# Two more pairs with P split and turned by the DMA, and the softmax sums turned with the last slot of P, in an attention and convolution kernel

## The chip, the cores and the metric

The kernel runs on one core of a Trainium2 chip. The metric is the device time of one execution in microseconds (us), as the median of three runs; lower is better. The engines are PE (matmul; PEld is its weight load), DVE, ACT and POOL (elementwise), and SP, which here only issues DMAs.

## What is computed

```python
q_n, k_n = rmsnorm(q, g_q), rmsnorm(k, g_k)            # 8 batches, 12 heads, 448 positions, 64 wide
scores = (q_n @ k_n.T) / sqrt(64)
attn = exp(scores - max(scores, -1))
attn = attn / (sum(attn, -1) + 1e-9)
x = (attn @ v) -> (8, 448, 768)                        # heads side by side
h = max(x @ w_in, 0)                                   # 768 -> 1024
conv = sum of 3 taps of conv_w over positions of h
out = (h * sigmoid(conv)) @ w_out                      # 1024 -> 768, float32
```

## The kernel before, in words

**Pairs.** The 96 heads are taken two at a time: pairs 0 to 47, six to a batch. For each pair, q and k are loaded, squared, summed, normalised (`rsqrt`, `apply_rms`) and turned; `scores` are multiplied into PSUM banks in seven slots of 128 query rows. For every slot `soft_max` (DVE, L999) takes the negated row maximum into a small tile, and `soft_exp` (ACT, L1007) writes P = exp(...) in float32 into one of four buffers `e`, and the row sum into a column of `rsum` (128 rows, 7 columns).

**Two ways for P.** P has to be turned before it can be multiplied with v. For a pair below `NV` = 10 it stays in float32: `p_transpose` (PE, L1038) turns each slot by four multiplications with the identity, 112 columns each; `p_evac` (a float32 copy, mostly on ACT, L438) moves it from the bank into `PT`; and `pv` (PE, L1120) multiplies in float32, eight products that PE carries out as 16 MATMULs. From pair `NV` on six of the seven slots (`TURNS`) are split into two float16 parts, `p_hi` (a cast) and `p_lo` (the rest, a subtraction on POOL or DVE, L450), in one of four buffers `ph`, and `p_turn` (SP, L1030) turns both by one DMA transpose. The last slot is still turned on PE, and then taken apart by `p_evac` (a cast) and `p_low` (DVE, L1055). Also v is split, by `v_hi` (mostly ACT) and `v_lo` (DVE, L1105), into `vp`, and `pv` takes three passes of eight products in float16, 24 MATMULs. `x_scale` then multiplies with the inverted sums: two instructions a pair on DVE below `NV` (L1134), one from there on (L1131).

**The sums.** After the last `soft_exp` of a pair, `sum_add` adds 1e-9 (POOL or DVE), `sum_step` inverts (DVE, L1065), `sum_transpose` (PE, L1068) turns the 128 x 7 tile into a bank of its own, `sum_evac` copies it to `rT`, and DMAs store it to DRAM (`sum_store`) and load it back, spread over the partitions (`sum_load`), as `rB`.

**The second half.** For each batch, `in_part` (PE, L1201) multiplies x, split in two float16 parts, with w_in; `in_relu`, `in_conv`, `in_tanh` and `in_gate` work on the bank (ACT and DVE); `in_hi` and `in_lo` split the result; `out_part` (PE, L1270) multiplies with w_out. The weights arrive as 64-bit numbers and are made into float32 in three DVE instructions a piece (`convert`), bounded (`bound`), and split (`split`, `rest`), all in the first part of the program.

**What sets the order.** Every step of the program has a number in a hand-held table (`ORDER`), and an engine for each elementwise step in another (`ENGINES`); `BANKS` names the PSUM bank of each step that takes one. The steps are issued in the order of the numbers, so each engine works through its own list in that order, without reordering. A step that waits holds up everything behind it on its engine.

Of the kernel before, what the change touches and what calls it, by code (L numbers as in the profile page):

```python
# [20 lines left out]
NF, NV, NQ = 10, 10, 10  # L21
# [10 lines left out]
    load_cw="3=6e4j",  # L32
    make_cw="8(",
    load="02080K0N0u0;0|1e1k2I2j2-2>3O4T4Y5D5Q5)626a6p7G7O7(868Z8v",
    convert=(
        "0A0D0G0g0i0t0!0)0-0}131S1P1Z1f1v1$1}1?2V2f2a2i2)2c2$42353a452}3P3^3h3r3|4C4F4O4A4D4I4<53"
        "5851555E5r5x5$5v5_5}6L6Q6W6f6i6l6|767B797E7J7p7w7!7*7}828K8O8T8j8l8q8`91999B9D9J"
    ),
    bound="0J0$0?2~2M2B2@2^4E4B44497q6X6d7T7L7k7<8h7)7n8a8e98969F9O",
    bound_max="4H9R",  # L40
    bound_turn="4J9U",
    bound_row="4L9X",
    bound_spread="4Q9i",
    scale="4S9l",
    in_factor="7N",
    split="4Z4o4*4~5p5(9p9y9<A5AKAsA<B8",
    rest="4i4w4^5a5y6Y9u9&9`ABARA$B2Bq",
    out_factor="A!",
    load_k=(
        "00040T0q1M2F2<3-4a5s6J7j7~9+AzCMDRElFuG-IKJXKnMCNIOGPvQ#R@T4UmVjWWY5Z$anbrcoe!fSgwh!j>j~"  # L50
        "mRmwo|p3"
    ),
    load_q=(
        "030B0a0#1t2R3j464d5+6=7m8^9>A&CQD_EyG6G`I#JjK*MGN`OUP@Q&SgTIU?VlX8YBZ(aqcScre%fVg|h&j_k3"
        "mqm!p0p7"
    ),
    square=(
        "060E0O0j151c2p2*4G4X606Z7>8A9tATCtC~E|FFGsHkJ_KXL%MuObO=R9RTTGTzVqW1YOYoapb6c;dHfRf<hfiD"
        "kVkkm_n9pTpb"
    ),  # L60
    square_sum=(
        "070I0b0p1G1j2+2?4V4n6E6u898YAHAmD0D6FEFZHfHwKaKhMAM!OkO{RKRdTYT*V;WIYYYva(bFdAdPfyg1hliL"
        "khkrnJnSpepo"
    ),
    rsqrt=(
        "090C0F0H0L0P0R0U0W0M0Q0S0V0X0c0f0h0k0d0m0o0s0y0&0*0<110x0z0(0+0=0_101A1E1s1u1y1#1%1;1=1^"
        "222{2|3033363D3F3I3f4t4v4x4(4-4=4@5B5F6(6+6<6?6{6}737M7R8g8k8o8s8x8$8+8=90A#A+A;A~B1BFBP"
        "BVBhDCDLDUDXDpDtDyD!D&FiFqFsF&F)F<F@F^F}H-H@H`H}I4ILITIdIhKtKuKwK&K_K~L1L7LDM;M=M?M_M|N1"
        "N2NENHP6PAPDPFPUPWPdPgPlRkRoRxR(R-R=R?R_S7T@T_T|U0U4U5U9UAUHWRWVWYWkWlWqWuW%W*Y=Y?Y_Y}Y~"
        "Z0Z2Z5Z7bNbPbSbfbhbibmbobsdXdadddmdzd%d?d_d`g8gCgFgKgLgOgQgUgYiSiViYiaibifigijipk!k#k&k*"  # L70
        "k=k@k_l7l9nZnandngnknlnnnqnvptpvpzp#p;p@p`q3q7"
    ),
# [73 lines left out]
    sum_store=(
        "2N3N3t5M5~6$7g8bAfBfD4DxF8GIHtIyJ@L9M3NLO;P$ROScTyU%W5X6YJZnazbQc<eEf+h8h=i}kBlimVoAo_qG"
# [1257 lines left out]
```

## Time and profile before

| what | value |
|---|---|
| median of three runs | 804.49 us (804.42 to 805.22) |
| the profiled execution's own time | 805.12 us |
| its span, first to last instruction | 803.3 us |
| PE busy | 780.5 us (97%) |
| DVE busy | 712.0 us (89%) |
| ACT busy | 637.5 us (79%) |
| POOL busy | 450.7 us (56%) |
| DMA queue that SP fills | 79.9% of 16 engines' span |
| granted TensorE clock | 0.998 |

The span is what the profile shows; the 1.8 us between it and the time lie around it. Busy shares are means over the whole program, and the stages differ: the weights are prepared in the first fifth, attention goes on to about 700 us, and the last 60 us belong to the second half of the last batch. Matmuls overlap, so the mean duration of one is longer than what it adds to the stream; busy time over the number of instructions, or the distance from one start to the next, is nearer to that.

### The profile page before, as it was taken

To read this page: it belongs to the slowest core of one execution; us is meant where nothing else is said; L and a number is where in the kernel's file an instruction comes from. 1 tells how busy PE (TensorE), PEld (TensorE's weight loads), DVE (VectorE), ACT (ScalarE), POOL (GpSimd) and SP (SyncE) were. 2 spreads that over 40 slices of the span, in tenths; PEclk is the share of its full clock that TensorE was granted. 3 is DMA by queue.
4 is the path that set the end of the run, shared out by engine and by line. 5 is a ranking of instruction groups with operands and counts; after the bars stand their busy time and mean duration, and the time that the engine had idled before them with its cause. 6 is when DMAs were issued, how large, how long until landed. Compare 5 with 4: busy or idle time off the path is not lost.

```text
span 803.3 us, 16861 instructions
## 1 busy us (share of the span) xinstructions
PE 780.5 (97%) x5564; PEld 421.6 (52%) x5564; DVE 712.0 (89%) x1489; ACT 637.5 (79%) x1542; POOL 450.7 (56%) x552
## 2 busy tenths in 40 slices
PE   3998999999999999999999999999999999999998
PEld 1545555555554555555555555555555555555554
DVE  7999999999999889998899988999999899992560
ACT  5999999997898777998788868998799767862221
POOL 2556246766478457766696646885487543530020
PEclk9999999999999999999999999999999999999999
DMA  8864653499998989999899999999999998846002
GB/s 246 236 193 116 172 179 101 97 186 208 187 199 183 195 177 209 194 182 195 188 188 199 200 181 199 207 190 197 191 189 180 209 196 182 160 91 150 12 1 79
DMA packets 345704, 137.46 MB, mean 171 GB/s; under 512 B 285376, under 2 KB 342032, under 8 KB 345616
## 3 DMA queue, kind: packets, MB, share of 16 engines
q1 hardware_dynamic: 345616, 136.37, 79.9%
q8 instruction: 44, 0.72, 0.4%
q14 instruction: 44, 0.36, 0.1%
HBM read 56.65 MB, written 11.18 MB: 84 GB/s over the span
## 4 chain that ended last, share of the span: by engine, by line
PE 55%; DVE 1%; ACT 1%; issue 1%; POOL 0%; ACTq 0%
PE bank L1270 21%; PE bank L1201 17%; PE bank L1120 7%; PE bank L993 7%; PE bank L1038 1%; PE bank L812 1%; ACT e L1007 0%; PE bank L1068 0%; DVE c L1221 0%; DVE ph L450 0%; POOL ph L450 0%; ACT PT L438 0%; ACT ph L438 0%; ACT sq L741 0%; ACT bank L1209 0%
## 5 line engine op out<-in xcount | busy, mean ns | idle before, releaser
L1201 PE MATMUL bank<-x,wi 128*128 128x448 f16 x1152 | 236.6, 353 | 0.8 <-DVE c L1231 0.6
L450 POOL TENSOR_TENSOR ph<-e,ph 128x448 f16<-128x448 f32 x139 | 148.8, 1073 | 93.9 <-ACT ph L438 60.9
L1270 PE MATMUL bank<-wo,gring 128*128 128x384 f16 (+1 forms) x1056 | 191.7, 327 | 0.0
L1201 PEld LDWEIGHTS <-wi 128*128 128x128 f16 x1152 | 110.1, 98 | 102.0 <-issue 12.8
L1270 PEld LDWEIGHTS <-gring 128*128 128x128 f16 (+1 forms) x1056 | 100.4, 99 | 65.1 <-issue 10.8
L993 PE MATMUL bank<-kT,qT 64*128 64x448 f16 (+3 forms) x1072 | 128.1, 390 | 3.8 <-ACT e L1007 2.2
L1120 PE MATMUL bank<-PT,vp 112*64 112x448 f16 x912 | 93.1, 354 | 0.0
L450 POOL TENSOR_TENSOR sq<-qkf,st 112x512 f32<-112x512 f32 x73 | 80.1, 1108 | 17.9 <-DVE st L773 7.2
L1221 DVE SCALAR_TENSOR_TENSOR c<-bank,cwb,c 128x447 f32<-128x447 f32 x128 | 85.8, 675 | 3.1 <-ACT c L442 2.1
L438 ACT CAST ph<-e 128x448 f16<-128x448 f32 x141 | 78.4, 561 | 2.1 <-DMA PT<-ph 2.0
L1120 PEld LDWEIGHTS <-vp 112*64 112x64 f16 x912 | 48.9, 110 | 41.0 <-issue 11.2
L1038 PE MATMUL bank<-ident,e 128*112 128x128 f32 x432 | 64.1, 281 | 0.0
L752 DVE TENSOR_REDUCE st<-sq 112x16 f32<-112x1024 f32 (+1 forms) x50 | 58.1, 1167 | 4.2 <-ACT sq L741 4.1
L450 DVE TENSOR_TENSOR ph<-e,ph 128x448 f16<-128x448 f32 x89 | 58.1, 655 | 2.8 <-POOL ph L450 1.2
L1038 PEld LDWEIGHTS bank<-ident,e 128*112 128x112 f32 x432 | 49.7, 136 | 20.0 <-ACT e L1007 5.6
L993 PEld LDWEIGHTS <-qT 64*128 64x128 f16 (+1 forms) x912 | 33.7, 97 | 49.4 <-issue 28.9
L442 ACT ACTIVATE c<-bank,vsc 128x384 f32<-128x384 f32 x45 | 25.8, 580 | 41.1 <-PE bank L1270 41.0
L450 POOL TENSOR_TENSOR gring<-c,gring 128x448 f16<-128x448 f32 x32 | 34.8, 1088 | 38.2 <-ACT gring L438 36.4
L741 ACT ACTIVATE sq<-qkf 112x1024 f32<-112x1024 f32 (+1 forms) x47 | 47.9, 1021 | 6.5 <-DMA qkf<-in_q_dram 4.3
L1227 ACT ACTIVATE c<-c 128x448 f32<-128x448 f32 x64 | 36.5, 573 | 17.3 <-DVE c L1221 13.7
L450 POOL TENSOR_TENSOR x<-x,x 128x448 f16<-128x448 f32 x34 | 37.9, 1116 | 21.7 <-DVE x L438 15.2
L450 POOL TENSOR_TENSOR qkf<-sq,qkf 112x512 f16<-112x512 f32 x35 | 42.5, 1213 | 9.9 <-DVE qkf L438 6.1
(1148 smaller groups left out, 1588.0 us busy)
## 6 DMA issues: line engine op xcount, KB each, us to landing
qkf<-in_k_dram SPq DMA_DIRECT2D x48, 224.0 KB
v<-in_v_dram SPq DMA_DIRECT2D x48, 224.0 KB
rB<-rd SPq DMA_DIRECT2D x96, 112.0 KB
out_dram<-c SPq DMA_DIRECT2D x56, 192.0 KB
wo<-in_moe_w_in_dram SPq DMA_DIRECT2D x12, 512.0 KB
gring<-in_moe_w_out_dram SPq DMA_DIRECT2D x16, 384.0 KB
qkf<-in_q_dram SPq DMA_DIRECT2D x24, 224.0 KB
qkf<-in_q_dram SPq DMA_DIRECT2D x48, 112.0 KB
```

Source lines behind the costliest of these rows:

```text
L438: (nc.scalar.copy if e == "ACT" else elementwise(e).tensor_copy)(dst, src)
L442: nc.scalar.activation(dst, src, AF.Copy, scale=scale)
L450: elementwise(e).tensor_tensor(dst, a, b, op=op)
L741: nc.scalar.activation(sq, x, AF.Square)
L752: nc.vector.tensor_reduce(st, sq, axis=AX.X, op=ALU.add)
L993: nc.tensor.matmul(ps[u][o, :S], lhs, rhs, start=(i == 0), stop=(whole(m) or i == 2),)
L1038: nc.tensor.transpose(ps[:PB, kt * P : (kt + 1) * P], e[:, kt * PB : (kt + 1) * PB], ident)
L1120: nc.tensor.matmul(ps[HALF[h], :S], lhs, rhs, start=(i == 0 and k == 0), stop=(i == pvs(n)[-1] and k == NB - 1),)
L1201: nc.tensor.matmul(ps[:, :S], wi[:, wl, c, fc * P : (fc + 1) * P], old("x", b * NP + c)[:, xl], start=(i == 0), stop=(i == 3 * NP - 1),)
L1221: nc.vector.scalar_tensor_tensor(c[:, dst], h[:, src], w[:, tap, fc : fc + 1], c[:, dst], op0=ALU.mult, op1=ALU.add)
L1227: nc.scalar.activation(c, c, AF.Tanh)
L1270: nc.tensor.matmul(ps[p0 : p0 + m, :NO2], g, wo[:, wl, fc, half * NO2 : (half + 1) * NO2], start=(i == 0), stop=(i == 3 * NFC - 1),)
```

## The change

`NV` goes from 10 to 8: pairs 8 and 9 take the float16 way too. `sum_transpose` goes. The buffers `e` become eight columns wider; `sum_step` writes the seven inverted sums behind the 448 columns of the last slot's P, and the last of that slot's four transposes takes 119 columns instead of 112, so that the sums come out in rows 112 to 118 of the same bank. `sum_evac` copies rows 96 to 118 of it, `sum_store` stores the seven. So in each pair the last slot's `p_transpose` now waits for `sum_step`. The row maxima lie in the columns of one tile (`tops`). The tables `ORDER`, `ENGINES` and `BANKS` are written anew.

```diff
-NF, NV, NQ = 10, 10, 10
+NF, NV, NQ = 10, 8, 10
...
-    split="A",
-    rest="VVVVVVVVVVGVVV",
+    split="AAAAAGAAAAAAAG",
+    rest="V",
...
-        tag: [const.tile([P, S], F32, name=f"{tag}{i}") for i in range(BUFS[tag])]
-        for tag in ("e", "c")
+        tag: [const.tile([P, w], F32, name=f"{tag}{i}") for i in range(BUFS[tag])]
+        for tag, w in (("e", S + 8), ("c", S))
...
+    tops = const.tile([P, BUFS["sst"]], F32, name="tops")
...
     def soft_max(n, j):
-        st = new("sst", (n, j), [P, 1], F32)
+        ring = rings.setdefault("sst", Ring(BUFS["sst"]))
+        i = ring.count % BUFS["sst"]
+        st = ring.put(("sst", (n, j)), tops[:, i : i + 1])
...
-            take("e", (n, j)), held["s", (n, j)][:, :S], AF.Exp, bias=old("sst", (n, j)),
+            take("e", (n, j))[:, :S], held["s", (n, j)][:, :S], AF.Exp, bias=old("sst", (n, j)),
...
         for kt in range(NB):
+            w = PB + (NS if j == NS - 1 and kt == NB - 1 else 0)
             nc.tensor.transpose(
-                ps[:PB, kt * P : (kt + 1) * P], e[:, kt * PB : (kt + 1) * PB], ident
+                ps[:w, kt * P : (kt + 1) * P], e[:, kt * PB : kt * PB + w], ident
             )
...
     def sum_step(n):
-        nc.vector.reciprocal(old("rsum", n), old("rsum", n))
-
-    def sum_transpose(n):
-        nc.tensor.transpose(
-            bank("t", ("r", n))[:NS, :P], old("rsum", n), ident
-        )
+
+        nc.vector.reciprocal(old("e", (n, NS - 1))[:, S : S + NS], old("rsum", n))
 
     def sum_evac(n):
-        copy(on["sum_evac", n], new("rT", n, [NS, P], F32), held["t", ("r", n)][:NS, :P])
+
+        copy(
+            on["sum_evac", n], new("rT", n, [P, P], F32)[96 : PB + NS],
+            held["t", ("p", n, NS - 1)][96 : PB + NS, (NB - 1) * P : NB * P],
+        )
 
     def sum_store(n):
-        queue("rd").dma_start(new("rd", n, [NS, P], F32, pD), old("rT", n))
+        queue("rd").dma_start(new("rd", n, [NS, P], F32, pD), old("rT", n)[PB : PB + NS])
```

**PE, the end of pair 0.** Below, PE's list before, up to the multiplication of pair 0 with v (`PT`, `v`); `rsum` is the tile of the sums.

```order
L1038 MATMUL bank_67<-ident,e_77 112x128 x4
L993 MATMUL bank_68<-kT_262,qT_280 128x448
L993 MATMUL bank_69<-kT_262,qT_280 128x448
L1038 MATMUL bank_72<-ident,e_74 112x128 x4
L1038 MATMUL bank_66<-ident,e_75 112x128 x4
L1068 MATMUL bank_71<-ident,rsum_222 7x128
L1120 MATMUL bank_67<-PT_259,v_190 64x448 x8
```

The same stretch of the changed kernel, whose line numbers are two to five lower:

```order
L1036 MATMUL bank_68<-ident,e_75 112x128 x4
L1036 MATMUL bank_67<-ident,e_76 112x128 x3
L1036 MATMUL bank_67<-ident,e_76 119x128
L988 MATMUL bank_70<-kT_253,qT_269 128x448
L988 MATMUL bank_73<-kT_253,qT_269 128x448
L988 MATMUL bank_68<-kT_253,qT_269 128x448
L988 MATMUL bank_69<-kT_253,qT_269 128x448
L1036 MATMUL bank_72<-ident,e_77 112x128 x4
L1036 MATMUL bank_66<-ident,e_74 112x128 x4
L1036 MATMUL bank_71<-ident,e_75 112x128 x4
L1118 MATMUL bank_67<-PT_262,v_216 64x448 x8
```

The row of the sums is gone; the last slot's fourth transpose has 119 rows out, and nine rows of other work (scores and the next pair's transposes) now stand between it and the multiplication.

**ACT, pairs 8 and 9.** ACT's list before, in the slots of pair 9: `e` is written, and each slot is copied from its bank into `PT`; the rows of `wo` split w_out.

```order
L1007 ACTIVATE e_75,rsum_1495<-bank_66,sst_(9_2_1556 128x448
L438 COPY PT_1586<-bank_69 112x4x128
L442 ACTIVATE wo_93<-wo_93,wsc 128x768
L1007 ACTIVATE e_76,rsum_1495<-bank_71,sst_(9_3_1594 128x448
L1227 ACTIVATE c_79<-c_79 128x448
L438 COPY PT_1586<-bank_68 112x4x128
L442 ACTIVATE wo_93<-wo_93,wsc 128x768
```

The changed kernel, at the end of pair 8:

```order
L432 CAST ph_87<-e_75 128x4x112
L631 ACTIVATE wo_93,wamax<-wo_93 128x384 x2
L1004 ACTIVATE e_74,rsum_1425<-bank_69,tops 128x448
L432 CAST qkf_1164<-sq_1247 112x512
L432 CAST ph_88<-e_74 128x4x112
L631 ACTIVATE wo_93,wamax<-wo_93 128x384
L1206 ACTIVATE bank_67<-bank_67 128x448
L432 COPY rT_1454<-bank_70 23x128
L432 CAST PT_1313<-bank_70 112x4x128
```

The copies from the bank have become casts into `ph`; only the last slot still comes from a bank, the sums beside it.

**SP, pair 8.** SP's list before holds no transpose of P in this place (the first one belongs to pair 10):

```order
L716 DMA qkf_1308<-in_k_dram 112x2x256
L616 DMA gring<-in_moe_w_out_dram 128x768 x2
L1076 DMA rd_1380<-rT_1375 7x128
L616 DMA gring<-in_moe_w_out_dram 128x768
L1082 DMA rB_1421<-rd_1380 64x448 x2
L890 DMA v_1444<-in_v_dram 112x2x256
```

and in the changed kernel:

```order
L611 DMA gring<-in_moe_w_out_dram 128x768
L1027 DMA_TRANSPOSE PT_1313<-ph_86 128x8x128
L1027 DMA_TRANSPOSE PT_1313<-ph_87 128x8x128
L1080 DMA rB_1348<-rd_1302 64x448 x2
L1027 DMA_TRANSPOSE PT_1313<-ph_88 128x8x128
L721 DMA qkf_1245<-in_q_dram 112x4x128
L885 DMA v_1385<-in_v_dram 112x2x256
```

Twelve transposes of P (240 in all instead of 228) have come in between the loads of w_out, q, k and v.

## Rows read from the trace of the kernel before

**Rows 1.** The page, part 1: busy us, share of the span, instructions.

```profile
PE 780.5 (97%) x5564; PEld 421.6 (52%) x5564; DVE 712.0 (89%) x1489; ACT 637.5 (79%) x1542; POOL 450.7 (56%) x552
```

**Rows 2.** Stretches: us, busy of PE, PEld, DVE, ACT, POOL, clock, DMA share, GB/s.

```profile
20.00:40.00 20.00, 18.83 (x123) 11.16 (x123) 19.56 (x45) 19.51 (x51) 10.79 (x17) 1.00 0.90 237
...
100.00:120.00 20.00, 19.93 (x122) 11.32 (x121) 19.43 (x52) 19.36 (x56) 9.64 (x13) 1.00 0.61 182
120.00:140.00 20.00, 19.94 (x120) 10.44 (x119) 19.62 (x48) 19.89 (x48) 13.28 (x17) 1.00 0.38 102
140.00:160.00 20.00, 20.00 (x122) 10.35 (x121) 19.69 (x40) 19.93 (x44) 15.63 (x16) 1.00 0.42 91
160.00:180.00 20.00, 20.00 (x145) 10.64 (x145) 19.83 (x38) 19.78 (x47) 13.17 (x15) 1.00 0.90 186
180.00:200.00 20.00, 20.00 (x161) 11.17 (x158) 18.30 (x43) 15.65 (x43) 13.71 (x16) 1.00 0.99 204
```

**Rows 3.** Groups of PE's instructions by line and shape: busy us, mean ns.

```profile
L1120 PE MATMUL bank<-PT,vp 112*64 112x448 f16 x912 | 93.1, 354 | 0.0
...
L1038 PE MATMUL bank<-ident,e 128*112 128x128 f32 x432 | 64.1, 281 | 0.0
...
L1120 PE MATMUL bank<-PT,v 112*64 112x448 f32 x160 | 32.3, 545 | 0.0
...
L1068 PE MATMUL bank<-ident,rsum 128*7 128x128 f32 x48 | 13.1, 273 | 0.3 <-DVE c L1231 0.2
```

**Rows 4.** PE's timeline near 400 us: start us, us, instruction, count.

```profile
402.07 0.27 PE L1068 MATMUL bank<-ident,rsum 128*7 128x128 f32 x1
402.18 0.73 PE L1201 MATMUL bank<-x,wi 128*128 128x448 f16 x3
...
404.26 0.60 PE L1038 MATMUL bank<-ident,e 128*112 128x128 f32 x4
404.70 1.86 PE L1201 MATMUL bank<-x,wi 128*128 128x448 f16 x9
```

**Rows 5.** PE's timeline near 31 us, pair 0.

```profile
30.78 0.27 PE L1068 MATMUL bank<-ident,rsum 128*7 128x128 f32 x1
30.98 3.23 PE L1120 MATMUL bank<-PT,v 112*64 112x448 f32 x16
```

**Rows 6.** The timeline near 170 us: pair 10's last slot on DVE.

```profile
170.43 0.68 DVE L1055 TENSOR_TENSOR PT<-bank,PT 112x512 f16<-112x512 f32 x1
170.64 1.88 PE L993 MATMUL bank<-kT,qT 64*128 64x448 f16 x18
```

**Rows 7.** Groups of ACT's instructions by line and shape.

```profile
L438 ACT CAST ph<-e 128x448 f16<-128x448 f32 x141 | 78.4, 561 | 2.1 <-DMA PT<-ph 2.0
...
L438 ACT COPY PT<-bank 112x512 f32<-112x512 f32 x68 | 38.3, 598 | 0.9 <-PE bank L1038 0.5
...
L899 ACT ACTIVATE vabs<-v 112x512 bf16<-112x512 f32 x29 | 18.3, 631 | 1.0 <-DVE vacc L896 0.7
...
L442 ACT ACTIVATE wi<-wi,wsc 128x1024 f16<-128x1024 f32 x6 | 7.1, 1182 | 0.0
```

**Rows 8.** Groups of DVE's instructions by line and shape.

```profile
L1055 DVE TENSOR_TENSOR PT<-bank,PT 112x512 f16<-112x512 f32 x38 | 26.0, 683 | 3.0 <-ACT PT L438 2.7
...
L901 DVE TENSOR_REDUCE vacc<-v 112x1 f32<-112x512 f32 x19 | 12.7, 680 | 0.2
```

**Rows 9.** The tile ph: duration ns min/median/max, first and last start us.

```profile
L1030 SPq DMA_TRANSPOSE PT<-ph x228: 1231/1264/2458, 153.7 to 733.1; - x114
...
L450 POOL TENSOR_TENSOR ph<-e,ph x139: 1027/1038/1676, 150.3 to 730.3; 128x448 f16<-128x448 f32 x139
L450 DVE TENSOR_TENSOR ph<-e,ph x89: 603/618/1379, 157.8 to 727.5; 128x448 f16<-128x448 f32 x89
```

**Rows 10.** The tile rsum: the sums of the pairs, duration ns min/median/max.

```profile
L1065 DVE RECIPROCAL rsum<-rsum x48: 178/192/202, 29.6 to 725.9; 128x7 f32<-128x7 f32 x48
...
L1062 POOL TENSOR_SCALAR rsum<-rsum x29: 242/243/1001, 25.7 to 693.6; 128x7 f32<-128x7 f32 x29
```

More of the change, by code (lines that the diff above doesn't have):

```diff
@@ L31 @@
     make_g="0Y",
[L32 to L34 removed]
+    load_cw="3R3X58",
+    make_cw="8i",
+    load="02080K0N0c0%0>1f1x2K2q2(393P4P4U5H5O5(5+6a6l787J7x7@8T8r",
     convert=(
[L36 to L39 removed]
@@ L40 @@
[L40 to L48, printed above, removed]
+        "0A0D0G0h0j0u0#0*0;0~1A1a1K1P1U1%1<1~1y1@2U2R2e2!2b2+3}333i3_3C3T433Z3?41474C4K45494F4_53"
+        "5C4+4?5J5w5z5$5y5!5&6E6P6W6U6Z6i6+6}72777B7E7h7l7s7y7#7<8C8J8O8h8k8n8%8;979B9N9Q"
+    ),
+    bound="0J0$0@3D2n282}37423~46447r6e6%6z8Z7i7e8s7g7n8U8!8c9F9J9W",
@@ L49 @@
+    bound_max="4E9Y",
+    bound_turn="4G9a",
+    bound_row="4I9f",
+    bound_spread="4L9k",
+    scale="4O9n",
+    in_factor="6T",
+    split="4V4k4*5F5x5^9s9-A1ALAbA`BCBW",
+    rest="4d4r565r5*6c9w9^ADARAlB7BIB)",
+    out_factor="A+",
     load_k=(
-        "00040T0q1M2F2<3-4a5s6J7j7~9+AzCMDRElFuG-IKJXKnMCNIOGPvQ#R@T4UmVjWWY5Z$anbrcoe!fSgwh!j>j~"
-        "mRmwo|p3"
+        "00040T0r1q2D363z4}5q6R7X7_9|AjCODdExF>G~IZJnK&MUM_OGPmQ^R(TSU$VhW{X|ZdabcJcfd)fKg@hjjQj("
+        "lUmMooo&"
     ),
@@ new lines @@
+        "s-t8u7uD"
+    ),
+    v_max="2Z7UDZLGR`Z+gboZ",
+    v_turn="2c7jE1LdSKZ=gmol",
+    v_row="2i7oEVLpSXZ@gqon",
+    v_spread="2r7tEdLxSta3gvos",
+    v_scale="2u7wEnL!Sva5gxov",
+    p_hi=(
+        "878M8l8o8_999S9$9{AJAQApA_BHBfBxB?C2CTCjCsC<D4DFDaDxD;D>EJEPEaE!E}F1FMFhFoF|G8GbGqG^G{HJ"
+        "HQHfHxH`IOIYIvI?JMJTJmJ&J=KFKGKjKxK;K^L9LXL#L;M4M5MLMhMkM!M<NRNVNsN^ODOOOfO(PEPOPtP(Q0QC"
+        "QQQgQ$R5RMRaRiRqR?S1SJSVSnS;S<T7TETbTxT-T~USUZUrV3V4VQVZV!W1WBWcWtW|X7XAXVXqX)Y7YEYXYgYv"
+        "Y=Y_Z8ZrZvZ~aIaaagasa&a}bAbBbab!b{c8cKcWc-dEdYdid=d>eCeMeoeyfDfUfZfof=f>gHgWgkg*h3hIhVhX"
+        "hyh)i8iEiSioiti{jLjTjrj<kFkIkikuk=l8lRlVlkl(m3m5mTmzm$m^n0nEnQnkn(o8oLocoho=pCpfpgpzp@qD"
+        "qTqpquq#q}r5rUror!r^s5sasfsvs(s~tGtStdtj"
@@ new lines @@
+        "qhq&q>r9rIrTrlr%sDsNsTsps?tAs}t6tatltut!"
+    ),
+    p_low="9iBSCuEHE_GFG*H}J)KzL^MiO6P?QtR!S%UDVLWqYJZOZ{bLc9dde-g7hBi4j6k(mCnXoTo`qjrzs_t_",
+    v_hi="7*8(BcDRE@F+GDHrJIKkL{MlMrORRDSCS=TvUqWvXSX-a9aYbgc#eUfWg;hhjzkBl_mnoyo+q+rXsLsm",
+    v_lo="7?8`CIE5FCF?GkJ2KbK~MQNLMxP8RSSkTuT)VOW<Y%YVaracb=c+ftfwhUhuj?kwmanfo%pIq{rmtotP",
+    qk_lo="9uA^C)D?EqFrGvHtJhKpL|MaN`PSQeReT8TpU|WfXbY+aFajc5d6eqfgh4hlj4k7mAmvn|pBqfrW",
+    q_hi="9m9OB(CrECEyG3HcI$K3LkL(NgOnPvR8SdTVUzV2XMY4Z&aNbocceXe%g?hsi)jElSmqn`o#qnrS",
@@ L275 @@
     convert="V",
-    bound="A",
+    bound="AAAAAVAAAAAAAAAAAAVAAAAAAAAA",
     bound_max="V",
@@ L307 @@
     p_evac=(
-        "AAAAAAAAAAAAAAAAAAAAAAAAAAAAAAAAVAAAAAAAAAAAAAAAAAAAAAAAAAAAAAAAAAVAAAAAAAAAAVAAAAAAAAAA"
-        "AAVAAAAAAAAAAAAAAAAV"
+        "AAAAAAAAAAAAAAAAAAAAAAAAAAAAAAAVAAAAAAAAAAAAAAAAAAAAAAAAAAAAAVAAAAVAAAAAAAAAAAAVAAAAAAAA"
+        "VAVVVAAV"
     ),
-    sum_add="GGGGGGVGGVGVVVGVGVVVGGGGGGGGVVGVGVGGGVGVGGVGVGVV",
+    sum_add="GGVGGGGGVGGGGVVGGGGGGVGGGGVGGGVGGGVVVGGGGVVGGGGV",
     sum_step="V",
-    sum_transpose="T",
-    sum_evac="AAVAVAVAVVAAVAAAAAAAAAAAAAAVAVAAAAAAAVAAAAAAAAVA",
+    sum_evac="VAVAVAVAAAAAAAAAAAAVVAVAVAAAAVVAVAVAVVAAAVAAVVVA",
     sum_store="S",
```

370 lines of the change are left out of this document (173 added, 197 removed).

## The prediction

> **What bounds the kernel now.** The page's shares come first: PE is busy 97% of the span, DVE 89%, ACT 79% [rows 1]. That reads as a kernel bound by PE, of which every instruction taken away would shorten the end. The table of stretches corrects it [rows 2]. From 20 to 180 us DVE and ACT are as full as PE: DVE idles 0.2 to 0.6 us in each 20 us shown there, ACT 0.1 to 0.6, and in the first of them PE idles more (1.2 us) than either. Here the weights are prepared beside attention. From 100 us on PE is full as well, because the second half of the first batch can fill its gaps. Only after 180 us do DVE (18.3) and ACT (15.7 of 20) come loose, and from there PE alone sets the end. So there are two parts: up to about pair 10 the elementwise engines set when the pairs are ready, behind it PE runs through without a gap. What PE saves in the first part comes back only if DVE and ACT are earlier too; what it saves in the second counts in full.
>
> **What PE loses and gains, all in all.** *Transposes of P.* Six slots of two pairs, four each: 48 go. One is 64.1 / 432 = 0.148 us of busy time [rows 3], or 0.44 / 4 = 0.11 us from start to start inside a stream [rows 4]; I take 0.135, since pairs 8 and 9 have neighbours of many kinds: -6.5 us. The rows of one group give 281 ns as the mean of one, but these overlap. *The sums' transposes.* 48 go. In a stream the next instruction starts 0.11 us later (402.07 to 402.18) [rows 4], before a float32 product 0.20 us later (30.78 to 30.98) [rows 5]; the mean duration is 273 ns [rows 3]. I take 0.13, near the first, which is the common case: -6.2 us, with 5.3 and 13.1 as ends. *Pairs 8 and 9 with v.* 32 float32 instructions go, 32.3 / 160 = 0.202 us each, and 48 in float16 come, 93.1 / 912 = 0.102 us each [rows 3]: -6.5 + 4.9 = -1.6 us. The seven more columns of one transpose in a pair cost nothing that I can price beside the 0.11 us of the whole instruction. Together PE has 14.3 us less to do.
>
> The Trainium skill ("TensorE: Matmul & The Clock Gate", Part 4) gives about 275 ns for a PE transpose in a kernel's context; the trace has that as a duration (281 and 273 ns), but starts stand 110 ns apart in a stream, and by the page's figure as a price the 96 transposes would be worth 26 us, an estimate that the busy time contradicts.
>
> **What DVE and ACT get.** I count both kernels' lists up to one place: the end of pair 10's work on P, its `p_low` on DVE, which ends at 170.43 + 0.68 = 171.1 us before; PE's next scores (170.64) stand right beside it [rows 6]. By the table's numbers, ACT's list ahead of it changes so: 12 more casts into `ph` at 0.56 us, 13 fewer copies into `PT` at 0.60, 4 more bounds of v at 0.63, 2 fewer splits of weights at about 1.18 [rows 7]; five other kinds change by two and eight by one, net eight more instructions, two of them short, the others at some 0.6 us: +4.2. Sum: 6.7 - 7.8 + 2.5 - 2.4 + 4.2 = +3.2 us. DVE's list: 5 more `p_lo` at 0.62 [rows 9], 2 more `p_low` at 0.68, 4 fewer bounds of v at 0.68 [rows 8], and single ones up and down that net to about +1.0: 3.1 + 1.4 - 2.7 + 1.0 = +2.8 us. Both are full there [rows 2], so pair 10 comes some 3.2 us *later*, not earlier, although PE has 8.2 us less to do ahead of it (6.5 + 1.6 + eleven sums at 0.13, less 1.3 us of scores and `out_part` that now stand ahead). PE will idle about 11 us more in this stretch.
>
> POOL gets seven more `p_lo` at 1.04 us by that place [rows 9], one more weight split and the rest of v of one pair; it is busy 13 of 20 us there [rows 2], so this is beside. SP issues twelve more transposes, at 1.26 us each [rows 9] 15 us, between 110 and 150 us, where the DMA share is 0.38 to 0.61 [rows 2] and SP holds no transposes of P before 153.7 [rows 9]: hidden in some 30 us of free DMA time; without that cover they would delay loads of q and k by up to 15 us.
>
> **The sum.** Behind that place PE had 803.3 - 171.1 = 632.2 us. Of its 14.3 us, 8.2 lie ahead, so 6.1 us lie behind (37 sums at 0.13 and the 1.3 us moved). End: 171.1 + 3.2 + 632.2 - 6.1 = 800.4, that is -2.9 us. The same count at pair 10's first product with v gives +3.3 us ahead and only the 37 sums, 4.8 us, behind: -1.5 us. I take the middle, **-2.2 us**. The profiled execution took 805.12 us, 1.8 over its span and 0.6 over the median of the runs; against itself that makes 802.9, against the median 804.49 - 2.2 = **802.3 us**. About 0.2% (1.6 us) is what a measurement of this kernel tells from no change: below 802.9 counts as faster, above 806.1 as slower.
>
> **Rivals.**
> *PE alone decides.* If DVE and ACT had slack that I do not see, or their waits shrank, all 14.3 us would come back: 790.2 us; half of it, 797.3. For it: the 97%. Against it: 160 us in which DVE is idle for some 2%. I give the whole 5% and the half 8%.
> *The gains cancel.* Lists that are longer by 3 us on two engines that feed each other can cost more than the longer one; 2 us more, and what is left is within a few tenths of nothing: about 804.3 us. 20%.
> *Slower: the last slot waits for the sums.* Before, only the small transpose waited for `sum_add` and `sum_step`; now the last slot's four do, and behind them everything on PE. From the last row sum it is 0.24 us on POOL and 0.19 us on DVE [rows 10], when these are free at once. The list puts other work in front, as at the end of pair 0, but DVE is full early on. If PE stands 2.2 / 48 = 0.05 us a pair the gain is gone; at 0.15 us a pair it is 802.3 + 7.2 = 809.5 us. For it: PE does not reorder matmuls. Against it: PE's waits for these sums before were 0.3 us in all [rows 3]. 10%.
> *Slower: DVE is held up by POOL.* DVE's `p_lo` takes 603 to 618 ns as a rule and once 1379, POOL's 1027 to 1676 [rows 9], and the small add on POOL 242 or 1001 [rows 10]: now and then one stands for about the length of the other's instruction. If each of the seven more `p_lo` on POOL held DVE for its whole 1.04 us, pair 10 would come 7.3 us later: 809.6 us. It decides from 0.3 us each. Against it: DVE's median is 15 ns from its minimum. 7%. The Trainium skill ("SBUF — State Buffer", Who interferes with whom) says that a DVE instruction with two inputs in SBUF and a GpSimd instruction that reads SBUF exclude each other for whole instructions, whichever came first; the longest rows agree, the medians say that it is rare here.
> *The change does not do what it says.* The lists show it done: 240 transposes on SP, no row of `rsum` on PE. No chance of its own.
>
> **How the numbers follow.** The forecast has 50%, with a range of 800 to 804 from the two places of the count and the ends of the prices (a sum's transpose at 0.11 us makes it 0.8 us less, at 0.27 some 5 us more). Three quarters of that lie below 802.9: 0.38. With both PE cases (0.13) and a little of the cancelling case, faster is 0.53. Same: 0.12 of the forecast, 0.16 of the cancelling case and 0.02 from the edges of the slow ones, 0.30. Slower: 0.17. For eight times in ten, 798.5 leaves out the whole PE case and most of the half, and 807.0 the heavier ends of the two slow rivals.
>
> **What would show it.** PE's busy time falls by about 14 us, to some 766, and its idle time between 80 and 180 us rises from under 1 us to about 11, its releasers being ACT's `e` and `PT` and DVE. DVE and ACT stay at 19.4 us or more in each 20 us up to 180. `p_low` of pair 10 ends near 174 us, and from 190 us on PE has no gap worth naming. The group of L1068 is gone; L1036 has 384 instructions. I am wrong if pair 10 ends before 171 us with PE's idle time unchanged (then PE alone decided), if the last slots' transposes show waits for `sum_step` of a few us in all, or if DVE's `p_lo` has a median well over 620 ns.

## The result, and the profile after

The change made the kernel **slower**: 811.94 us, median of 4 runs (810.80 to 813.12), beside 804.86 us for the kernel before on the same chip; ratio 1.0086, 95% interval 1.0074 to 1.0098. The forecast was 802.3 us. The profiled execution of the changed kernel took 813.12 us, its span is 811.3 us, against 805.12 and 803.3 before: 8.0 us more span. It is the slowest of its four, so some 0.9 us of the 8.0 is scatter between executions: the medians lie 7.1 us apart.

The page's first part, after; the row it answers to is [rows 1]:

```profile
PE 775.4 (96%) x5484; PEld 415.3 (51%) x5484; DVE 720.6 (89%) x1505; ACT 640.3 (79%) x1533; POOL 466.7 (58%) x562
```

PE has 80 instructions less and is busy 5.1 us less, not 14. The groups of PE's instructions by shape, after (beside [rows 3]):

```profile
L1118 PE MATMUL bank<-PT,vp 112*64 112x448 f16 x960 | 99.4, 358 | 2.0 <-DMA v<-in_v_dram 2.0
...
L1036 PE MATMUL bank<-ident,e 128*112 128x128 f32 x336 | 51.6, 279 | 3.9 <-ACT PT L432 1.9 <-ACT e L1004 1.3 <-ACT c L436 0.3
...
L1118 PE MATMUL bank<-PT,v 112*64 112x448 f32 x128 | 25.8, 545 | 0.4 <-ACT PT L432 0.4
...
L1036 PE MATMUL bank<-ident,e 128*119 128x128 f32 x48 | 13.4, 278 | 0.3 <-DVE e L1064 0.3
```

The work did go: 64.1 + 13.1 + 32.3 us of transposes and float32 products became 51.6 + 13.4 + 25.8, and 93.1 of float16 became 99.4, together 12.4 us less. That the page's busy time falls by 5.1 only is because a matmul counts as busy for some 0.28 to 0.36 us while the next may start 0.11 to 0.19 us behind it: a stall shorter than the rest shows as busy. I therefore also added up PE's steps (four transposes, three products of `in_part`, ...) from the start of one to the start of the next, and took the 40th percentile of its kind as a step's own length. By that measure PE's own work fell from 754.6 to 741.9 us, 12.7 less, and its standing (the rest of the time from its first step to its last) rose from 33.7 to 54.0 us, 20.3 more. Such sums hold to a microsecond or so: with the steps cut in another way the work falls by some 11.3 us. Of the 20.3, 14.8 lie between 80 and 200 us and 6.1 between 440 and 610 us; elsewhere the two kernels stand about alike.

The stretches after (columns as in [rows 2]; below them the two parts that the prediction cuts the span into, of before and then of after, cut at the end of pair 10's `p_low`):

```profile
100.00:120.00 20.00, 18.26 (x108) 9.57 (x108) 19.11 (x49) 19.26 (x51) 11.78 (x13) 1.00 0.45 129
120.00:140.00 20.00, 17.96 (x96) 7.66 (x93) 19.42 (x51) 19.89 (x52) 12.09 (x15) 1.00 0.98 198
140.00:160.00 20.00, 16.17 (x92) 8.00 (x90) 17.79 (x30) 17.25 (x37) 17.65 (x21) 0.91 0.76 147
160.00:180.00 20.00, 18.63 (x134) 9.38 (x131) 20.00 (x38) 19.86 (x50) 14.68 (x15) 1.00 0.88 165
180.00:200.00 20.00, 20.00 (x160) 10.97 (x159) 19.29 (x42) 17.79 (x44) 11.53 (x15) 1.00 0.93 190
```

```profile
0.00:171.11 171.11, 153.19 (x921) 82.62 (x922) 163.62 (x382) 158.73 (x386) 92.90 (x126) 0.99 0.63 169
171.11:803.30 632.19, 627.29 (x4647) 339.02 (x4643) 548.37 (x1109) 478.76 (x1157) 357.77 (x427) 1.00 0.85 172
```

```profile
0.00:177.68 177.68, 149.44 (x880) 77.16 (x881) 167.75 (x384) 162.44 (x397) 100.23 (x128) 0.99 0.76 182
177.68:811.30 633.62, 625.96 (x4606) 338.11 (x4604) 552.90 (x1123) 477.89 (x1137) 366.49 (x435) 1.00 0.86 171
```

These four rows hold the whole result. Pair 10's `p_low` on DVE, at 170.43 us before [rows 6], now stands here in the timeline:

```profile
177.00 0.68 DVE L1053 TENSOR_TENSOR PT<-bank,PT 112x512 f16<-112x512 f32 x1
```

It ends 6.6 us later (177.68 for 171.11), where I had 3.2. DVE was busy 4.1 us more by then (167.75 for 163.62) and idle 2.4 us more; ACT was 3.7 us more busy and 2.9 more idle. Behind that place the kernel takes 633.6 us instead of 632.2: 1.4 us more, where I had 6.1 less. So, against the first of the prediction's two counts (2.9 us less), 3.4 us of the miss lie ahead of pair 10 and 7.5 us behind it.

### The profile page after: what moved, and what is told of

Same layout as the page of the kernel before. It is cut to its first block, busy times and chain, and to the rows that moved or that the text cites. A ratio compares the mean times of both kernels' runs of the same rounds, so it can differ in the third digit from the quotient of the medians.

```text
span 811.3 us, 16767 instructions
## 1 busy us (share of the span) xinstructions
PE 775.4 (96%) x5484; PEld 415.3 (51%) x5484; DVE 720.6 (89%) x1505; ACT 640.3 (79%) x1533; POOL 466.7 (58%) x562
## 5 line engine op out<-in xcount | busy, mean ns | idle before, releaser
L1004 ACT ACTIVATE e<-bank,tops 128x448 f32<-128x448 f32 x336 | 212.8, 637 | 58.3 <-DVE tops L996 33.7
L444 POOL TENSOR_TENSOR ph<-e,ph 128x448 f16<-128x448 f32 x150 | 161.4, 1080 | 84.3 <-ACT ph L432 43.9
L996 DVE TENSOR_REDUCE tops<-bank 128x1 f32<-128x448 f32 x336 | 198.3, 613 | 9.1 <-PE bank L988 8.3
L1118 PE MATMUL bank<-PT,vp 112*64 112x448 f16 x960 | 99.4, 358 | 2.0 <-DMA v<-in_v_dram 2.0
L432 ACT CAST ph<-e 128x448 f16<-128x448 f32 x159 | 88.2, 562 | 0.4
L444 POOL TENSOR_TENSOR sq<-qkf,st 112x512 f32<-112x512 f32 x69 | 75.4, 1101 | 20.6 <-DVE st L768 6.7
L1004 ACT ACTIVATION_READ_ACCUMULATOR e<-bank,tops 128x1 f32 x336 | 68.5, 204 | 0.0
L1036 PE MATMUL bank<-ident,e 128*112 128x128 f32 (+1 forms) x384 | 57.5, 279 | 4.2 <-ACT PT L432 1.9
L1036 PEld LDWEIGHTS bank<-ident,e 128*112 128x112 f32 (+1 forms) x384 | 44.9, 140 | 26.6 <-ACT e L1004 7.2
L436 ACT ACTIVATE c<-bank,cwb 128x448 f32<-128x448 f32 x56 | 35.4, 635 | 19.1 <-DVE bank L1208 17.9
```

The lines of the kernel that those rows point to most:

```text
L432: (nc.scalar.copy if e == "ACT" else elementwise(e).tensor_copy)(dst, src)
L444: elementwise(e).tensor_tensor(dst, a, b, op=op)
L996: nc.vector.tensor_reduce(st, held["s", (n, j)][:, :S], axis=AX.X, op=ALU.max, negate=True)
L1004: nc.scalar.activation(take("e", (n, j))[:, :S], held["s", (n, j)][:, :S], AF.Exp, bias=old("sst", (n, j)), accum_out=old("rsum", n)[:, c ...
L1036: nc.tensor.transpose(ps[:w, kt * P : (kt + 1) * P], e[:, kt * PB : kt * PB + w], ident)
L1118: nc.tensor.matmul(ps[HALF[h], :S], lhs, rhs, start=(i == 0 and k == 0), stop=(i == pvs(n)[-1] and k == NB - 1),)
```

## The experiments

Theory A: the split's own elementwise work on DVE, ACT and POOL brings pair 10 late. B: PE stands at the last slots for the inverted sums. C: neither edit, but the order with its waits. D: the DMA turns are not hidden. E: PE is not the bound behind 180 us, others hold nearly the same pace. Times are medians; "PE idle" is a stretch less PE's busy time in it.

### Each half alone, in the order of before

Three kernels were put into the order of before, changed only as far as the new steps want. **e1**, the ride alone (the changed code with `NV` = 10):

```diff
-NF, NV, NQ = 10, 8, 10
+NF, NV, NQ = 10, 10, 10
```

Where `sum_step` stood behind the last slot's transpose, both were moved toward each other (`sum_step` to at most 12 places behind the last exponential, the transpose behind it); ten PSUM banks had to be chosen anew.

> The kernel before, with one half of the change: the inverted sums ride in the last slot's transpose, the 48 single transposes are gone, pairs 8 and 9 stay as they were and the order stays that of before (sum_add, sum_step and the last slot's transpose moved only as far as the new dependency wants). If the split of pairs 8 and 9 is what costs (theory A): PE has some 5 to 6 us less work and is the bound behind 180 us, so 800 to 802 us. If the ride costs (theory B: PE stands at the last slot's transposes or behind the e buffers that are held longer): 805 us or more, with small PE stalls all along from 200 us on. If neither edit but the new order costs (theory C): 800 to 802 us, as with A.

Measured: 827.5 us, ratio 1.0277 (1.0263 to 1.0290). **e2**, the split alone (the code of before with `NV` = 8; `p_hi` and `p_lo` where the transpose stood, `p_turn` where its evacuation stood):

```diff
-NF, NV, NQ = 10, 10, 10
+NF, NV, NQ = 10, 8, 10
-pair 8, slot j: p_transpose (PE), p_evac (ACT)
+pair 8, slot j: p_hi (ACT or POOL), p_lo (POOL or DVE), p_turn (SP)
```

> The kernel before, with the other half alone: pairs 8 and 9 in float16, their P turned by the DMA, put into the order of before where their transposes and evacuations stood; the sums keep their own transpose. Theory A: DVE, ACT and POOL are full up to 180 us, pair 10 comes 4 to 7 us later, 807 to 811 us. Theory B: 800 to 805 us. Theory C: 803 to 806 us.

Measured: 822.0 us, ratio 1.0215 (1.0202 to 1.0228). **e3**, both edits at once, the changed code in the order of before:

> Both halves in the order of before, hardly adapted, in place of the new table. Theory A: the sum of the two runs above, some 804 to 807 us. Theory B: as the change, 810 us or more. Theory C: under 805 us, and the new table is at fault for what the change took more.

Measured: 844.1 us, ratio 1.0487 (1.0470 to 1.0504). None of the theories had numbers like these. Each half costs 17 to 23 us where the order is not made for it, and the two add up: the new tables (order, engines and banks together), which I had blamed under C, earn 32 us. *Where* they lose is told apart cleanly. PE idle, from the table of stretches, in 80 to 200, 200 to 430 and 430 to 610 us: before 0.45, 1.23 and 0.06; e1 2.47, 5.22 and 5.44; e2 17.03, 1.24 and 0.06; the change 9.56, 1.02 and 3.00. From 80 to 200 us, e2 and then the change:

```profile
80.00:200.00 120.00, 102.97 (x624) 51.13 (x623) 114.81 (x229) 102.17 (x246) 72.20 (x85) 0.94 0.69 156
```

```profile
80.00:200.00 120.00, 110.44 (x698) 55.60 (x697) 115.56 (x243) 113.46 (x278) 74.70 (x84) 0.99 0.77 169
```

Up to 610 us, the split loses in one stretch, ahead of pair 10, and nothing behind it, and the ride loses a little everywhere, where every pair pays. In e1 part of that is theory B, in the list of PE's waits from 200 to 430 us (who waits, for whom, us in total, times, longest):

```profile
PE bank L1036 <- DVE e L1064: 1.5, 4, 0.5
PE bank L1198 <- DVE c L1228: 0.8, 1, 0.8
PE bank L1267 <- ACT e L1004: 0.8, 1, 0.8
```

L1036 is the transpose, L1064 `sum_step`. In the change this wait is 0.3 us in all (the group of 48 above).

### The change's waits, one by one

**e4.** Once the first scores are under way, the longest wait of PE in the change is 2.0 us at 152 us, where the profile names a load of v. PE's timeline of the change there:

```profile
154.31 3.82 PE L1118 MATMUL bank<-PT,vp 112*64 112x448 f16 x24 [2.01 <-DMA v<-in_v_dram]
158.06 0.91 PE L1036 MATMUL bank<-ident,e 128*112 128x128 f32 x4
158.91 1.31 PE L988 MATMUL bank<-kT,qT 64*128 64x448 f16 x12
160.96 4.13 PE L1198 MATMUL bank<-x,wi 128*128 128x448 f16 x21 [0.74 <-DVE PT L1053]
```

Pair 8's products read no such load; they write bank 1, which `qk_lo` of pair 11 on DVE frees at 154.26 us. The edit exchanges banks 1 and 3 in the table from there on:

```diff
-bank of pv(8, 0): 1    bank of p_transpose(9, 6): 3
+bank of pv(8, 0): 3    bank of p_transpose(9, 6): 1
```

> The changed kernel with two PSUM banks exchanged from pair 8's products with v on, and nothing else: these products then take a bank that was freed earlier than qk_lo of pair 11. If their 2.0 us wait at 152 us is for that qk_lo on DVE (ended at 154.26 us, PE went on at 154.31), the wait goes, DVE and ACT idle less behind it, and the end comes 1 to 2 us earlier: 810 to 811 us. If the wait is for the load of v that the profile names, it stays at 2.0 us and the time at 811.9.

The same place in e4:

```profile
151.74 2.46 PE L1118 MATMUL bank<-PT,vp 112*64 112x448 f16 x24
154.13 0.65 PE L1036 MATMUL bank<-ident,e 128*112 128x128 f32 x4
156.53 1.31 PE L988 MATMUL bank<-kT,qT 64*128 64x448 f16 x12 [1.74 <-DVE c L1228]
159.18 5.47 PE L1198 MATMUL bank<-x,wi 128*128 128x448 f16 x21 [1.34 <-DVE PT L1053]
```

The wait was for the bank: it is gone, and pair 8's products start 2.6 us earlier. What follows is only 1.8 us earlier, since a new wait of 1.74 us (for `in_gate` on DVE) and a longer one for `p_low` (1.34 us instead of 0.74) take its place, and the end does not move: 812.8 us, 1.0092 (1.0078 to 1.0107). Here, in a stretch where DVE and ACT are nearly full as well, the stall was handed on.

**e5.** Theory B in the change itself; the last slot's transpose carries seven columns of ones in place of the sums:

```diff
-        nc.vector.reciprocal(old("e", (n, NS - 1))[:, S : S + NS], old("rsum", n))
+        x = old("rsum", n)
+        nc.vector.reciprocal(x, x)
```

> The changed kernel, but the inverted sums stay in their own tile and the last slot's transpose carries seven constant columns instead, so that it no longer waits for sum_add and sum_step; every instruction and the order are the same, the output is not divided by the sums. If the wait of the last slots for the sums makes the small PE stalls behind 200 us (theory B; between 430 and 610 us PE loses 6 us more than before): 805 to 808 us. If these stalls come from the order of the other work, with the sums ready in time (theory C): 811 to 812 us.

811.4 us, 1.0078 (1.0065 to 1.0091), within the interval of the change. The new order has the sums ready in time, and theory B falls for the change, though not for e1.

**e8, e9.** Theory D. e8 issues each of the turns of pairs 8 and 9 twice:

```diff
-        nc.sync.dma_start_transpose(
+        for _ in range(2 if n < 10 else 1):
+            nc.sync.dma_start_transpose(
```

> The changed kernel with each of the twelve DMA transposes of pairs 8 and 9 issued twice, 15 us more of SP and DMA work between 119 and 154 us, where the DMA share is 0.76 to 0.98. If the transposes are hidden, as the prediction had it: 811.5 to 813 us. If they delay loads that PE, DVE or ACT then wait for (theory D): 815 us or more.

844.2 us. By its own expectation this speaks for D, but the experiment was badly made: the second turn writes the place of the first, so SP waited for the first to land, 28.4 us in twelve waits, and ACT for the four buffers of `ph`:

```profile
SPq L1028 <- DMA PT<-ph: 28.4, 12, 4.6
...
ACT ph L432 <- DMA PT<-ph: 22.8, 8, 4.9
```

It shows only that a stop of SP's queue there reaches the end: 28.4 us of waiting and twelve more issues, and 32 us more time. e9 takes the turns away:

```diff
         c = slot(n, j)
+        if n < 10:
+            return
         nc.sync.dma_start_transpose(
```

> The changed kernel without the twelve DMA transposes of pairs 8 and 9 (their products read old numbers in their place); casts, p_lo and products stay. If these transposes are hidden (the prediction's step 4): 811 to 812.5 us, pair 10's p_low ends at 177 us or later. If SP's queue and the DMAs delay what PE, DVE and ACT wait for (theory D): pair 10 ends 2 us earlier or more and the time is 807 to 810 us.

812.0 us, 1.0096 (1.0081 to 1.0111). Pair 10's `p_low` ends at 176.2 us, 1.5 earlier and between the two forecasts; in e5 and e11, which leave the work of this stretch as it is, it ends at 177.4 and 177.2. The end stays: as far as the end goes, the turns are hidden as the prediction had it.

**e11.** From 440 to 500 us a chain starts at SP. It waits 4.2 us for POOL before it turns pair 29's slot 3; behind it stand the sums of pair 28 and v of pair 34, for which DVE and ACT then wait (the change's timeline):

```profile
457.04 2.30 SPq L1027 DMA_TRANSPOSE PT<-ph  x1
...
465.09 0.63 DVE L1129 TENSOR_TENSOR x<-bank,rB 128x448 f32<-128x448 f32 x1 [1.05 <-DMA rB<-rd]
465.66 0.63 ACT L894 ACTIVATE vabs<-v 112x512 bf16<-112x512 f32 x1 [2.46 <-DMA v<-in_v_dram]
```

The edit moves four loads ahead of that turn in SP's order:

```diff
+sum_load(28, 0), sum_load(28, 1), v_load(34), v_load(35)
 p_turn(29, 3)
-sum_load(28, 0)
 p_turn(29, 4)
-sum_load(28, 1), v_load(34), v_load(35)
```

> The changed kernel, and on SP's queue at 455 us the two sum_load of pair 28 and the v_load of pairs 34 and 35 stand ahead of the turn of pair 29's slot 3, for whose p_lo on POOL SP waits 4.2 us. If loads held up behind that wait start the stalls of 440 to 500 us (DVE waits 1.1 us for the sums, ACT 2.5 us for v, PE loses some 3 us more than before): 809 to 811 us. If the stalls come from elsewhere: 811.5 to 812.5 us.

811.3 us, 1.0077 (1.0065 to 1.0090): PE idle from 430 to 610 us falls from 3.00 to 1.83 us, and the median by 0.6 us, which this measurement does not tell from nothing. So it is one of several causes of the idle time there, and what it is worth at the end is open.

### The added work of pairs 8 and 9

**e6** leaves out the twelve `p_lo` (nine stand on POOL and three on DVE; its expectation miscounts them):

```diff
         ph = old("ph", (n, j))
+        if n < 10:
+            give("e", (n, j))
+            return
         binary(
             on["p_lo", n, j], ph[:, 1, :, :PB],
```

**e7** does that and e5's edit, **f3** leaves out `p_hi` in the same way too, and **e12** has all twelve `p_lo` on POOL, where they stand.

> The changed kernel without the twelve p_lo of pairs 8 and 9 (seven or eight on POOL, four or five on DVE); what is turned for the lower half is stale, the products are done as before. If DVE's and POOL's added work is what brings pair 10 late (theory A), pair 10's p_low ends 3 us earlier or more (174 us or less, from 177.7) and the end comes as much earlier: 807 to 809 us. If the place of the waits in the order decides (theory C), less than 1 us: 811 to 812 us.

> Both of the two edits above. Theory A and B together: 801 to 805 us, below the kernel before. If either edit alone gave nothing: 811 to 812 us, and the loss is in the order.

> The changed kernel without the twelve p_hi and the twelve p_lo of pairs 8 and 9 (zeros are turned and multiplied; turns and products stay). If the elementwise work of the split is what brings pair 10 late (theory A): p_low of pair 10 ends at 172 us or earlier (177.7 in the change, 171.1 before), and the time is 804 to 807 us. If it is the order with its waits (theory C): pair 10 ends at 175 us or later, 809 us or more.

> The changed kernel with all twelve p_lo of pairs 8 and 9 on POOL (three stood on DVE). If DVE's list is what brings pair 10 late (theory A): 1 to 2 us earlier, 810 to 811 us. If POOL, 17.7 of 20 us busy at 140 to 160 us, is what DVE and SP wait for: later, 813 us or more.

e6: 810.2 us, 1.0066 (1.0050 to 1.0082). e7: 810.5, 1.0073 (1.0054 to 1.0092), so nothing on top of e6. f3: 809.3, 1.0056 (1.0041 to 1.0071). Pair 10's `p_low` in e6 and then in f3:

```profile
173.64 0.68 DVE L1056 TENSOR_TENSOR PT<-bank,PT 112x512 f16<-112x512 f32 x1
```

```profile
172.99 0.68 DVE L1058 TENSOR_TENSOR PT<-bank,PT 112x512 f16<-112x512 f32 x1
```

Of the 6.6 us, 4.0 go with the split's casts and differences (177.0 to 173.0): theory A has the larger part of the delay. With `p_lo` alone 3.4 us go in e6, but in e7, which leaves out the same twelve, only 2.2 (`p_low` starts at 174.80): a place in one execution is good to about a microsecond. Of f3's 4.0 us the end gets 2.6 (by the two intervals, 1 to 4), and f3 still takes 4.5 us more than before. In f3 DVE's busy time up to pair 10 falls by 0.7 us only, its idle time by 3.3:

```profile
0.00:173.67 173.67, 148.59 (x880) 76.95 (x881) 167.03 (x381) 158.68 (x388) 90.29 (x116) 1.00 0.76 186
```

In these executions the work costs by the waits that it makes more than by its length. e12 took 812.6 us, 1.0099 (1.0084 to 1.0114), pair 10 at 180.1 us: fewer instructions on DVE, and later. Its DVE instructions are longer; the next part has why.

### DVE held by POOL

e2 shows it best. Its timeline, DVE and POOL, at two places:

```profile
125.84 2.03 POOL L450 TENSOR_TENSOR ph<-e,ph 128x448 f16<-128x448 f32 x2
125.94 2.15 DVE L577 TENSOR_SCALAR wo<-gring 128x384 int32<-128x384 int32 x1
...
143.04 1.03 POOL L450 TENSOR_TENSOR gring<-c,gring 128x448 f16<-128x448 f32 x1
143.06 1.83 DVE L673 SCALAR_TENSOR_TENSOR wo<-wo,wsc 128x768 f16<-128x768 f32 x1
```

A `convert` that takes 0.35 us as its median takes 2.15, until just behind POOL's two `p_lo`; a `rest` of 1.0 us that starts 20 ns behind POOL's instruction takes 0.83 us more. The rows of `rest` by duration (min/median/max) and of `square_sum`, a reduction, in the same stretch of e2:

```profile
L673 DVE SCALAR_TENSOR_TENSOR wo<-wo,wsc x7: 1005/1199/1847, 140.4 to 174.2; 128x768 f16<-128x768 f32 x7
```

```profile
L752 DVE TENSOR_REDUCE st<-sq x4: 1205/1210/1215, 114.0 to 156.2; 112x16 f32<-112x1024 f32 x4
```

Added up over all kinds, what DVE's instructions ahead of pair 10's `p_low` take over their usual lengths (the 25th percentile of the same step and shape) is 2.4 us before, 3.0 in the change, 6.9 in e12 and 11.4 in e2. The Trainium skill ("SBUF — State Buffer", Who interferes with whom) has DVE and GpSimd share a pair of ports that whoever issues first holds for the whole instruction, and names `tensor_reduce` as free of it on trn2; both agree with these rows, and in each of the four `square_sum` a POOL instruction was running beside it. **g1** is e2 with all twelve `p_lo` on DVE (`ENGINES`, `p_lo`: G to V for pairs 8 and 9):

> The split alone in the order of before (as e2, 822.0 us), with all twelve p_lo of pairs 8 and 9 on DVE instead of nine on POOL. If DVE held up by POOL is what cost there: DVE's list grows by 9 times 0.61 = 5.5 us, its instructions lose some 8 us of what they took over their usual lengths, pair 10's p_low ends earlier than in e2 (186.9 us), and the time is 816 to 820 us. If it was the length of DVE's list: 825 us or more.

819.6 us, 1.0188 (1.0174 to 1.0202), pair 10 at 187.7 us. The excess falls from 11.4 to 6.5 us, and DVE's list grows by 5.5: at pair 10 it cancels. So the hold is real and costs 5 us of DVE's time there, but it isn't what the 17 us hang on. What they hang on was not found. From 100 to 190 us of e2 SP's turns wait 9.8 us for POOL's `p_lo`, and the granted clock is 0.83 from 120 to 140 us and from 160 to 180.

### What PE's time is worth

**e10** adds to the change, and **f2** to the kernel before, one transpose in each pair, without a wait; **f1** takes the sums' 48 away from the kernel before (`sum_transpose` takes its bank and issues nothing).

```diff
+        if j == NS - 1:
+            nc.tensor.transpose(ps[:PB, :P], e[:, :PB], ident)
         for kt in range(NB):
```

> The changed kernel with one more PE transpose in each pair, 48 in all, that writes again what the first of the last slot's writes: PE's saving by the ride is taken back without any change to a wait. If PE is the bound behind 200 us: some 5 us more, 816 to 818 us. If other engines set the pace there and PE's saving comes back as stalls (theory E): 812 to 814 us.

> The kernel before without its 48 transposes of the inverted sums (the evacuation copies what the bank held, so the output is divided by other numbers); nothing else is changed or moved. If PE is the bound behind 180 us: 799 to 800.5 us, 5 us less. If the other engines hold the pace nearly as much (theory E): 803 to 804.5 us.

> The kernel before with 48 more transposes, one in each pair ahead of the last slot's four, writing what the first of these writes again. If PE is the bound: 809 to 811 us. If there were slack on PE: 805 to 807 us.

From start to start, f1's work is 5.2 us less than before, f2's 4.8 more, and e10's 4.8 more than the change's. The ends: f1 802.2 us, 0.9965 (0.9953 to 0.9977), 2.8 us less; f2 808.5, 1.0043 (1.0031 to 1.0055), 3.5 more; e10 813.3, 1.0100 (1.0086 to 1.0114), 1.4 more. By their intervals f1 gives 1.9 to 3.8 us and f2 costs 2.5 to 4.4. So in the kernel before 2.8 of 5.2 us reach the end when PE's work shrinks and 3.5 of 4.8 when it grows. In the change it is 1.4 of 4.8; the ratios of e10 and of the change differ by 1.1 us, with an interval from nothing to 2.6. Pair 10's `p_low` starts at 170.44 us in f1 and 170.61 in f2, as before: ahead of it these eleven transposes, some 1.2 us, are worth nothing, which is the prediction's first part. The other 37 lie behind it, some 4.0 us of f1's 5.2 and 3.7 of f2's 4.8, and there 2.8 and 3.5 of them reach the end: in the kernel before, most of PE's work counts in that part. The stretch from 430 to 610 us, of the kernel before, of the change and of e10:

```profile
430.00:610.00 180.00, 179.94 (x1362) 97.18 (x1360) 167.66 (x344) 152.25 (x370) 121.71 (x144) 1.00 1.00 193
```

```profile
430.00:610.00 180.00, 177.00 (x1316) 94.45 (x1313) 162.16 (x335) 147.27 (x356) 122.00 (x146) 1.00 0.97 193
```

```profile
430.00:610.00 180.00, 178.68 (x1341) 95.76 (x1340) 163.93 (x339) 148.87 (x359) 122.55 (x146) 1.00 0.96 194
```

With the transposes back PE idles 1.32 us there instead of 3.00, and DVE and ACT get more done in the same time. This is theory E for the change: most of what PE saves there, it stands.

### Two ways to the gain without the waits

**f4** rides the sums in the order of before only where they are ready anyhow:

```diff
+RIDE = (2, 7, 10, 11, 12, 17, 27, 28, 31, 43, 45, 47)
-            w = PB + (NS if j == NS - 1 and kt == NB - 1 else 0)
+            w = PB + (NS if n in RIDE and j == NS - 1 and kt == NB - 1 else 0)
```

> The kernel before in its own order, with the sums riding in 12 of the 48 pairs only (2, 7, 10, 11, 12, 17, 27, 28, 31, 43, 45 and 47), those in which sum_step stands ahead of the last slot's transpose or up to 4 places behind it. If PE is the bound and these waits are nothing: 12 times 0.11 to 0.13 us, 803.4 to 803.7 us. Where the evacuations now stand in other places, and if theory E holds: 804.5 to 806 us.

809.9 us, 1.0070 (1.0051 to 1.0089). Some evacuations had to follow their transposes to other places and the `e` buffers are held longer; PE idle rises by 2.1 us up to 80 us and by 2.7 from 430 to 720 us. **g2** has the DMA store the sums by row:

```diff
-        queue("rd").dma_start(new("rd", n, [NS, P], F32, pD), old("rT", n))
+            queue("rd").dma_start(
+                new("rd", n, [NS, P], F32, pD).rearrange("t p -> p t"), old("rsum", n)
+            )
```

> The kernel before without the sums' transposes and without their 48 evacuations: the DMA stores the sums from their tile by row, 896 single numbers of 4 bytes in each pair (rsum has four buffers for two). If the DMAs have the room: 800 to 803 us, by f1's 2.8 us and a little for 48 times 0.26 us less on ACT and DVE, and it beats both kernels. If so many small writes take the DMAs' time, whose share is 0.94 to 1.0 from 180 to 600 us, the loads come late: 810 us or more.

1081.8 us. 896 writes of 4 bytes in a pair fill the DMAs (the queue's packets, MB, share, and the chain that ended last):

```profile
q1 hardware_dynamic: 388720, 136.38, 90.8%
...
DMA 52%; PE 15%; DVE 9%; ACT 6%; POOL 6%; issue 5%; SPq 4%; DVEq 0%; ACTq 0%; POOLq 0%
```

Neither beats the kernel before, which stays the fastest of those that leave nothing out.

## Why the prediction was wrong

*What bounds the kernel: nearly right in the old order, wrong in the new one.* Ahead of pair 10 PE's work counts for nothing: f1 and f2 move pair 10 by 0.2 us at most. Behind it "PE alone sets the end" held for most of it in the kernel before (2.8 of some 4.0 us in f1, 3.5 of 3.7 in f2). The step that failed is to carry this over to another order: "behind it PE runs through without a gap", and what PE saves there "counts in full". I read it from PE's 20.00 of 20 us and DVE's 18.3 [rows 2]. But full means only that nothing stops PE in this order, as long as it is this slow. In the change PE idles 3.00 us from 430 to 610 us where it idled 0.06 before, and of e10's 4.8 us the end takes 1.4: DVE, ACT and the waits between them stand close behind PE.

*What PE loses: right.* 14.3 us forecast, 11 to 13 measured from start to start. Its busy time did not fall to 766 us as I had it, but to 775.4, since short stalls count as busy.

*What DVE and ACT get: the counts right, the delay half of what came.* I had +2.8 us for DVE's list and +3.2 for ACT's; they came to 4.1 and 3.7 us of busy time, DVE's with 0.6 us of POOL's holding in it. The step that failed is "both are full there, so pair 10 comes some 3.2 us later": it took the longer list for the delay. DVE also idled 2.4 us more, for PE's scores, for POOL's steps of `rsqrt` and for the sums, and from 140 to 160 us neither was full any more (DVE 17.79 us, ACT 17.25, where I had at least 19.4). That longer lists wait for each other more is my reading of it. Pair 10 came 6.6 us later.

*POOL's additions and SP's turns hidden.* For the end, the turns are (e9). POOL's additions are probably not: with three more `p_lo` on POOL and three fewer on DVE (e12) pair 10 comes 2.4 us later, though DVE has some 1.9 us less on its list. e6 can't tell the two engines apart, since it takes `p_lo` from both.

*Behind the place, 6.1 us less: the largest term that failed.* It came to 1.4 us more. Own work was some 4 us less there, but PE stood 6.1 us more between 440 and 610 us. Not for the sums (e5). Loads queued behind a turn that waits for POOL make some of it (e11: idle 3.00 to 1.83 us). Some of it is PE being early: with the transposes back it idles 1.32 us (e10). What else sets these stalls in the new order was not settled, and so their cause stays open in the main. One rival was not tried: the DMA share from 430 to 610 us is 1.00 before and 0.97 in the change, which may leave loads in a new order little room.

*The rivals.* "The last slot waits for the sums" holds in e1, where the order doesn't provide for it, and not in the change. "DVE is held up by POOL" holds in e2 (11.4 us of it) and e12, and is worth 0.6 us in the change, where the median of DVE's `p_lo` is still 618 ns. "The gains cancel" was nearest: it is what happened, and it went on past zero. The price that no rival named is the order: both halves in the old one cost 39 us (e3), and the new tables take back 32.

## What to carry to other kernels

A row of 100% for one engine says who is last now, not that its work comes back in full when it shrinks: take a known piece away without a wait (f1) or add one (f2) before building on it; here 5.2 us were worth 2.8, and after the change 4.8 were worth 1.4, with nothing to 2.6 as the interval. In a kernel whose order was made for its present durations, count an edit in a stretch with several full engines at more than the longer list (here 6.6 us for 4.1), and expect any single wait that you take away there to come back as the next one (e4).

## What the runs showed of the hardware that I had not expected

- A stall can cost PE twice. After the 2.0 us wait at 152 us the granted clock is 0.90 from 152 to 156 us and 0.67 from 156 to 160, so partly the lower of its two levels, and pair 8's 24 products take 3.82 us; without the wait, in e4, they take 2.46. The clock falls in e4 too, but behind its own waits: it is 0.81 from 156 to 160 us and 0.76 from 160 to 164.
- A one-input `tensor_scalar` of 0.35 us on DVE stood for two POOL instructions in a row, 2.15 us in all (e2).
- A wait for several semaphores that the profile puts down to a load can be for a PSUM bank. In the change, at 154.31 us, the load's last packets landed after PE had gone on, and the bank's reader had ended 0.05 us before; with another bank the wait was gone (e4).
- 896 DMA writes of 4 bytes in each of 48 pairs, in place of the transposes and their evacuations, cost 277 us on a kernel of 805 us, with that queue's packets taking 90.8% of the DMA engines' span (g2).
